# 48 more first-layer steps behind the last product, in eight groups that read their columns in different orders and from different begins

## The chip, the cores and the metric

The kernel runs on one core of a Trainium2 chip. Times are device microseconds of that core; lower is better. The engines are called as the profile calls them: PE (TensorE, with PEld for its weight loads), DVE (VectorE), ACT (ScalarE), POOL (GpSimd) and SP (SyncE, which issues DMAs here).

## The reference

A depthwise convolution over time is followed by a layer with a hard-swish gate:

```python
w = softmax(weight)                      # 8 heads x 7 taps
y[b, s, d] = sum_k w[head(d), k] * x_padded[b, s + k, d]   # 8 x 4096 x 192
h = y.reshape(32768, 192) @ w_in         # 192 x 2048
g = h * clip(h + 3, 0, 6) / 6
out = g @ w_out                          # 2048 x 192
```

All results are float32.

## The kernel before

The 32768 tokens are cut into 32 blocks of 1024, and a block into two halves of 512 columns. The 192 channels are laid on 96 partitions times two parts, so that with `y_own` and `y_other` two times 64 rows (`D2`) of TensorE's array are filled: rows 0 to 63 with one token half, rows 64 to 127 with the other.

**First layer** (`first_layer`, and `products` at L436 to L446). For each of 8 chunks of 128 hidden channels (twice, for the two groups) and each of three thirds (`s`) there are three passes, (high, high), (low, high) and (high, low). Weights and `y` are each kept as a high and a low part in the type fp32r, and `PASSES` names which parts meet. One **step** is one round of the inner loop over `k`: two matmuls that use 64 rows each, 128 weight columns and 512 moving columns, and write two neighbouring banks of PSUM. Each matmul comes with a weight load. `relu` on ACT (L315) and `gate` on DVE (L319) take the banks out.

**Second layer** (`second_layer`). It computes `g @ w_out` by sums and products of quarter matrices, in column tiles of 32 (`tile_position=(0, j * QS)`), so that four streams of f32 matmuls (L582, recorded by the helper `matmul`) run beside each other. Its order is written out by hand: `put` and `do` give each event a time on one of four streams, and the events are issued in order of that time. It takes three of the four PSUM slots (two banks each), `d, e, b, c, a, x_`, and the two banks `ends` of the fourth. In the last block (`last`) `end_lower` and `end_upper` turn the final rows and store them through the queues of SP, ACT and POOL.

**PSUM slots.** `free_slots` is the list of slots that are not taken. At the end of `second_layer` the three are given back behind the one that stayed, in this order:

```python
        free_slots.extend(ours[n] for n in (0, 2, 1))
```

so that behind the last block `free_slots[1]` is the slot of `d` and `e`.

**Weights of the first layer.** `w_in_parts` (L122) are two tiles, the high and the low part, with 8 x 3 x 128 = 3072 float32 columns per partition. They are written once in the first stage (L229 and L230) and then only read.

**The whole.** The first block is prepared in the first stage, with convolution taps on PE (`pe_tap`, L923: f32, 128 rows, 512 columns that begin at column k of `x0`), and its second layer is done plainly (L330). Blocks 1 to 31 follow in the loop over `i`, each a first layer and a second layer. TensorE's program is in the order in which the code issues it; all of this stands under `manual_schedule`. At the end of the program (L1162) all engines meet twice: each drains and counts up a semaphore, POOL waits for the count and lets the others go.

Of the kernel before, what the change touches and what calls it, by code (L numbers as in the profile page):

```python
# [1132 lines left out]
            left = second_layer(i, between)  # L1133


# [1 line left out]
_INS = ['x', 'weight', 'moe_w_in', 'moe_w_out']  # L1137
_OUTS = [((32768, 192), 'float32')]
# [28 lines left out]
```

## Time and profile before

| what | value |
|---|---|
| runs of the kernel | 2195.53, 2195.55, 2195.72 us; median 2195.55 |
| the profiled execution | 2195.85 us |
| its span, first to last instruction | 2194.1 us |
| granted TensorE clock | 1.000 |
| first-layer matmuls (L442) | 9216, in 4608 steps |
| second-layer matmuls (L582), largest group | 5720 |
| the last store's landing | about 2192.2 us |

The profile records each instruction's start and end. Matmuls overlap, and their ends are modelled; so the pace of TensorE is read from the distance between starts and not from the length of one. Groups of instructions have their line, engine, operation, output and inputs, shape and number. PEld are the weight loads, which run beside the matmuls of the step before. Entries whose engine ends in q (SPq, POOLq, PEldq) are records of an engine's sequencer: waits, drains and the issue of DMAs.

### The profile page before, as it was taken

To read this page: it belongs to the slowest core of one execution; us is meant where nothing else is said; L and a number is where in the kernel's file an instruction comes from. 1 tells how busy PE (TensorE), PEld (TensorE's weight loads), DVE (VectorE), ACT (ScalarE), POOL (GpSimd) and SP (SyncE) were. 2 spreads that over 40 slices of the span, in tenths; PEclk is the share of its full clock that TensorE was granted. 3 is DMA by queue.
4 is the path that set the end of the run, shared out by engine and by line. 5 is a ranking of instruction groups with operands and counts; after the bars stand their busy time and mean duration, and the time that the engine had idled before them with its cause. 6 is when DMAs were issued, how large, how long until landed. Compare 5 with 4: busy or idle time off the path is not lost.

```text
span 2194.1 us, 53702 instructions
## 1 busy us (share of the span) xinstructions
PE 2185.0 (100%) x23086; PEld 1565.5 (71%) x23086; DVE 1976.1 (90%) x1871; ACT 1270.9 (58%) x1761; POOL 1012.9 (46%) x859
## 2 busy tenths in 40 slices
PE   9999999999999999999999999999999999999998
PEld 5577777777777777777777777777777777777776
DVE  8889899889899898998989988999989999999987
ACT  7456565565655665555656556565566565565654
POOL 3445543355433555334554335553355543455433
PEclk9999999999999999999999999999999999999999
DMA  7366556756567665666655675656666566755564
GB/s 166 66 119 100 97 99 111 128 90 107 97 111 121 103 109 92 109 112 121 98 97 100 112 126 91 106 97 113 120 107 106 91 109 112 122 96 97 100 104 63
DMA packets 329821, 231.80 MB, mean 106 GB/s; under 512 B 208816, under 2 KB 293296, under 8 KB 329584
## 3 DMA queue, kind: packets, MB, share of 16 engines
q0 software_dynamic: 98752, 122.35, 36.6%
q1 hardware_dynamic: 229320, 105.73, 23.9%
q8 instruction: 181, 2.97, 0.6%
q10 hardware_dynamic: 1512, 0.30, 0.1%
q14 instruction: 56, 0.46, 0.1%
HBM read 31.72 MB, written 25.17 MB: 26 GB/s over the span
## 4 chain that ended last, share of the span: by engine, by line
PE 99%; ACT 0%; DVE 0%; POOL 0%; issue 0%; POOLq 0%; DVEq 0%
PE psum L582 49%; PE psum L442 47%; PE psum L330 2%; PE psum L923 0%; PE psum L931 0%; ACT g L315 0%; DVE results L409 0%; POOL w_in L230 0%; ACT scale L207 0%; ACT sig L204 0%; POOL out_dram L356 0%; ACT sig L210 0%; POOL sig L221 0%; DVE xt L832 0%; ACT w_in L229 0%
## 5 line engine op out<-in xcount | busy, mean ns | idle before, releaser
L582 PE MATMUL psum<-g,w_out 128*32 128x512 f32 (+1 forms) x5720 | 1023.7, 508 | 0.0
L315 ACT ACTIVATE g<-psum,half 128x1024 f32<-128x1024 f32 x512 | 571.3, 1116 | 313.5 <-PE psum L442 311.3
L582 PE MATMUL psum<-s,w_out 128*32 128x512 f32 (+1 forms) x3272 | 735.6, 570 | 0.9 <-DVE results L409 0.9
L319 DVE SCALAR_TENSOR_TENSOR g<-g,psum 128x1024 f32<-128x1024 f32 x512 | 609.1, 1211 | 134.3 <-ACT g L315 133.9
L540 POOL TENSOR_TENSOR s<-g 128x256 f32<-128x256 f32 x248 | 257.2, 1037 | 750.9 <-DMA out_dram<-results 639.6
L582 PEld LDWEIGHTS psum<-g,w_out 128*32 128x32 f32 x5720 | 421.0, 110 | 171.5 <-issue 61.6
L442 PE MATMUL psum<-y,w_in 64*128 64x512 f32 x4608 | 534.3, 388 | 0.4
L442 PE MATMUL psum<-y_other,w_in 64*128 64x512 f32 x4608 | 528.7, 386 | 0.0
L442 PEld LDWEIGHTS psum<-y,w_in 64*128 64x128 f32 x4608 | 428.6, 184 | 120.9 <-issue 26.0
L442 PEld LDWEIGHTS psum<-y_other,w_in 64*128 64x128 f32 x4608 | 431.6, 184 | 90.7
L1006 DVE SCALAR_TENSOR_TENSOR y<-x,c_sb,y 128x1536 f32<-128x1536 f32 x156 | 305.1, 1956 | 1.9 <-ACT y L1003 1.8
L582 PEld LDWEIGHTS psum<-s,w_out 128*32 128x32 f32 x3272 | 227.5, 110 | 106.3 <-issue 54.0
L582 PE MATMUL psum<-g,w_s 128*32 128x256 f32 x1488 | 289.3, 379 | 0.0
L389 POOL TENSOR_TENSOR s<-g 128x1024 f32<-128x1024 f32 x93 | 236.9, 2715 | 0.4 <-DVE g L319 0.4
L582 PE MATMUL psum<-z,w_s 128*32 128x256 f32 x992 | 235.1, 380 | 0.0
L389 DVE TENSOR_TENSOR s<-g 128x1024 f32<-128x1024 f32 x124 | 187.5, 1531 | 1.1
L582 PEld LDWEIGHTS psum<-g,w_s 128*32 128x32 f32 x1488 | 149.9, 110 | 31.9
L582 PE MATMUL psum<-s,w_s 128*32 128x256 f32 x744 | 170.7, 379 | 0.0
L482 ACT ACTIVATE z<-g 128x512 f32<-128x512 f32 x186 | 142.5, 766 | 18.4 <-DVE g L319 18.4
L409 DVE TENSOR_TENSOR g<-g 128x1024 f32<-128x1024 f32 x124 | 143.6, 1219 | 1.1
L409 DVE TENSOR_TENSOR results<-psum,results 32x256 f32<-32x256 f32 (+2 forms) x221 | 107.9, 488 | 39.6 <-PE psum L582 34.2
L389 DVE TENSOR_TENSOR g<-g 128x2048 f32<-128x2048 f32 x62 | 139.4, 2286 | 1.0
(114 smaller groups left out, 2335.2 us busy)
## 6 DMA issues: line engine op xcount, KB each, us to landing
y_other<-y SPq DMA_DIRECT2D x124, 384.0 KB, 5.1
z<-g POOLq DMA_DIRECT2D x93, 512.0 KB, 5.6
z<-z POOLq DMA_DIRECT2D x62, 512.0 KB, 5.4
out_dram<-results SPq DMA_DIRECT2D x375, 64.0 KB, 2.6
y<-x POOLq DMA_DIRECT2D x30, 768.0 KB, 9.0
x<-in_x_dram SPq DMA_DIRECT2D x53, 388.5 KB, 7.3
g<-g POOLq DMA_DIRECT2D x31, 512.0 KB, 6.3
g<-in_moe_w_in_dram SPq DMA_DIRECT2D x16, 192.0 KB, 5.8
```

The lines of the kernel that those rows point to most:

```text
L315: nc.scalar.activation(r6, h, ACT.Relu, bias=half[:], scale=1.0 / 6.0)
L319: nc.vector.scalar_tensor_tensor(out=g_, in0=g_, scalar=1.0, in1=h, op0=ALU.min, op1=ALU.mult)
L330: lambda p=p: nc.tensor.matmul(out=bank[j * QS : (j + 1) * QS, tokens], lhsT=w_out[:, p, w, cols], rhs=x[:, p, tokens], start=(first and p ...
L389: engine.tensor_tensor(out=o[:, r], in0=a[:, r], in1=b[:, r], op=op)
L409: nc.vector.tensor_tensor(out=out, in0=x, in1=y, op=op)
L442: nc.tensor.matmul(out=psum[:, 2 * slot + k], lhsT=r32(w_in_parts[wn][r, c, s]), rhs=r32(y_other[0][r, yn, s] if group else y_own[yn][r, s ...
L482: nc.scalar.mul(to, x, sign)
L540: engine.tensor_tensor(out=o, in0=p, in1=q, op=op)
L582: nc.tensor.matmul(out=out, lhsT=w, rhs=x, start=start, stop=True, tile_position=(0, j * QS), skip_group_check=True,)
L1006: nc.vector.scalar_tensor_tensor(out=y[:], in0=taps_of(k), scalar=c_sb[:, k : k + 1], in1=y[:], op0=ALU.mult, op1=ALU.add,)
```

## The change

Behind the loop over the blocks, 48 steps are added: eight groups of six, and in each step the two matmuls of 64 rows. The weights are always the same 128 columns of the high part, from column 24 on. The moving operand is 512 columns of the low part, which begin at column 24 plus `ahead`, in the order that `form` gives. Without a form the 512 columns are read one after the other. With `by_line` the columns are seen as runs of 16 (64 bytes), and the read goes over every b-th run, b times with another first run: with b of 4, 2 or 8 it steps over 256, 128 or 512 bytes from one run to the next. The last form reads every sixteenth column, 32 of them, sixteen times. The results are written into both banks of `free_slots[1]`, are sums of nothing else (`start` and `stop` are set in each), and are read by nobody. What is computed before stays as it is.

```diff
+        high, low = (w[:].rearrange("p c s f -> p (c s f)") for w in w_in_parts)
+        aligned = 24
+        spare = 2 * free_slots[1]
+
+        def columns(r, ahead, form):
+            c = low[r, aligned + ahead : aligned + ahead + N]
+            if form is None:
+                return c
+            pattern, sizes = form
+            return c.rearrange(pattern, **sizes)
+
+        by_line = "p (j b a) -> p b j a"
+        for ahead, form in (
+            (0, None),
+            (0, (by_line, dict(b=4, a=16))),
+            (0, (by_line, dict(b=2, a=16))),
+            (0, (by_line, dict(b=8, a=16))),
+            (32, None),
+            (48, None),
+            (16, (by_line, dict(b=4, a=16))),
+            (0, ("p (j a) -> p a j", dict(a=16))),
+        ):
+            for _ in range(6):
+                for k in range(2):
+                    r = slice(k * D2, (k + 1) * D2)
+                    nc.tensor.matmul(
+                        out=psum[:, spare + k], lhsT=r32(high[r, aligned : aligned + P]),
+                        rhs=r32(columns(r, ahead, form)),
+                        start=True, stop=True, skip_group_check=True,
+                    )
```

## Prediction

> **What bounds the kernel now.** I read the page first, its parts 1 and 4.
>
> ```profile
> span 2194.1 us, 53702 instructions
> PE 2185.0 (100%) x23086; PEld 1565.5 (71%) x23086; DVE 1976.1 (90%) x1871; ACT 1270.9 (58%) x1761; POOL 1012.9 (46%) x859
> PE 99%; ACT 0%; DVE 0%; POOL 0%; issue 0%; POOLq 0%; DVEq 0%
> ```
>
> TensorE is busy from end to end and makes up 99% of the chain that ended last. So what TensorE is given in the middle lengthens the span one for one. The change gives it work at the very end, though, where this share says nothing: there I need the last microseconds. The timeline of TensorE has its last products:
>
> ```profile
> 2187.12 0.39 PE L582 MATMUL psum<-s,w_out 128*32 128x256 f32 x3
> 2187.14 0.38 PE L582 MATMUL psum<-g,w_out 128*32 128x256 f32 x1
> 2187.34 0.39 PE L582 MATMUL psum<-s,w_out 128*32 128x256 f32 x3
> 2187.36 0.38 PE L582 MATMUL psum<-g,w_out 128*32 128x256 f32 x1
> ```
>
> Columns are start and length in us. The last product begins at 2187.36 and ends, as modelled, at 2187.73. The span ends at 2194.07, so 6.3 us follow in which TensorE has nothing to do. The chain, in order of time, and the records of the kernel's last line (L1162, where the engines meet) say what fills them:
>
> ```profile
> 2187.75 0.49 POOL out_dram L356
> 2188.24 0.09 issue
> 2188.33 0.58 POOL out_dram L356
> 2188.91 0.78 POOLq L1162
> 2189.69 0.53 POOL out_dram L356
> ```
>
> ```profile
> L1162 SPq EVENT_SEMAPHORE  x10: 17/28/1780, 2190.2 to 2194.0; - x10
> L1162 POOLq DRAIN  x3: 46/93/4281, 2188.8 to 2193.6; - x3
> L1162 SPq DRAIN  x3: 7/7/7, 2192.5 to 2193.3; - x3
> L1162 PEldq DRAIN  x2: 13/786/1560, 2186.3 to 2193.4; - x2
> ```
>
> (Shortest, median and longest in ns, then first and last start.) The last rows of the output are transposed and stored until 2190.2; SP then waits 1.78 us for stores to land, and its drain ends at 2192.54. GpSimd's first drain takes 4.281 us, from 2188.78 to 2193.06. TensorE's drain ends at 2187.84, 0.10 behind its last product. All engines are counted into one meeting that GpSimd closes: its wait begins at 2193.11, and 0.96 us later, with a second meeting in between, the span is over. So **TensorE arrives 5.2 us before the meeting**. That is the cover for whatever is put behind its last product.
>
> **The change, part by part.** It adds 48 steps. Each is two matmuls of 64 rows, 512 columns and 128 weight columns, with two weight loads: 96 matmuls and 96 loads, all on TensorE. It adds no DMA, no eviction and no store, and removes and moves nothing. All of it stands behind the last product in TensorE's program, so nothing is queued behind it but TensorE's drain.
>
> *Does the first one wait?* Its banks are those of the first of the three slots that the last block took, `d` and `e`. Their last readers are ACT's copies around L740 and L705 and DVE's at L409, from 2171.2 to 2173.1 in the timeline, 14 us before. `high` and `low` have been in place since the first 64 us. I cost the waits at nothing; without that cover the price would be what is left of such a copy, 0.4 us at most.
>
> *What is one step?* The first layer's steps have the same shape and number type. The timeline of TensorE inside and at the begin of a first layer:
>
> ```profile
> 2121.71 3.11 PE L442 MATMUL psum<-y,w_in 64*128 64x512 f32 x26
> ```
>
> ```profile
> 499.09 0.62 PE L582 MATMUL psum<-s,w_out 128*32 128x512 f32 x3
> 499.21 0.59 PE L582 MATMUL psum<-g,w_out 128*32 128x512 f32 x1
> 499.73 1.20 PE L442 MATMUL psum<-y,w_in 64*128 64x512 f32 x8
> ```
>
> 26 matmuls are 13 steps. Less the last one's own 0.386 and the 3 ns between the two of a step, 2.72 us hold 12 intervals: **226.5 ns a step**, and the starts in the trace say 226 or 227 in nearly all of 4608. At the begin it is slower: the last product of L582 started at 499.21 and takes 0.43 for its 512 columns, so the first step at 499.73 comes 0.09 later than the next product would have. The steps then start 337, 236, 228, 232 and 231 ns apart before the even pace holds; every later block shows the same five.
>
> *The sum with eight groups at this pace.* The last product has 256 columns and rounds of it start 0.215 apart, so the first new step starts at 2187.36 + 0.21 + 0.09 = 2187.66. Five slow intervals are 1.26 and 42 at 226.5 ns 9.51, so the last one starts at 2198.44 and ends 0.39 later, at 2198.83. The drain follows at +0.10, the meeting closes 0.04 behind it (as behind GpSimd's drain now), and 0.96 remain: 2199.93. Against 2194.07 that is **+5.9 us**: 11.1 us of TensorE's time, 5.2 of which lie beside the stores. SP may have to wait for the last added matmul before its drain, as nobody else reads its bank; from SP's last wait to the end of its drain it is 0.13 now, so at most 0.1 more. The stores themselves now have over 6 us to spare.
>
> A rule of the Trainium skill bears on the step (TensorE: Matmul & The Clock Gate, section "Wait — 56ns, not 53.3ns?"): once warm, matmuls start their columns divided by 2.4 GHz plus some 2.5 ns apart, 215.7 ns for 512. The row has 226.5, and the row decides; by the rule the sum would be 0.5 us less.
>
> *What do order and begin of the columns change?* No matmul in this trace reads its columns in another order, so I bound it. Groups 1, 5 and 6 read 512 neighbouring columns and differ in where they begin by 128 and 192 bytes. The nearest rows are the convolution taps on TensorE (L923), each one column further on than the one before: their matmuls start 428 to 433 ns apart with no more to it. Between nothing and 5 ns a step; I take nothing (12 steps would make 0.06 us). Groups 2, 3, 4 and 7 (the last begins 64 bytes further on) read runs of 16 columns (64 bytes) with 64 to 448 bytes skipped between them. Lower bound: the f32 products pass 512 columns in 429 ns; were a step twice as fast it would take 214.5, 12 less than it does, and an order that loses those 12 would give back 0.3 us over 24 steps. Upper bound: such a read goes at the pace of the f32 products, 429, which is 4.9 us over 24 steps. I take 226.5: if the 12 ns are lost at 32 changes from one 64-byte run to the next, 0.375 ns each (an estimate from these two rows), these groups change just as often. Group 8 takes every sixteenth column, so each column lies in another run than the one before. By that estimate 512 changes cost 192 ns, giving 406; the nearest row is the f32 pace, 429. Bounds: 226.5 below, and above it the 857 that a whole tap takes on L923 (two matmuls of 428). I take 429, **6 steps × 202 ns = +1.2 us**.
>
> The skill has a rule on this read, too (SBUF — State Buffer, in the box on cachelines; Advanced Engine Details and Errata, "SBUF Cachelines"): SBUF gives full bandwidth only where at least two accesses in a row fall into one 16-byte line. It speaks against group 8 alone, since runs of 64 bytes meet it, and states no price; no run here shows it yet.
>
> **Sum:** 5.9 + 1.2 = 7.1 us. The profiled execution took 2195.85, 1.75 beyond its span, and the median of the runs shown is 2195.55, 0.30 less; what lies around the span doesn't change. 2195.55 + 7.1 = **2202.6 us**, 0.32% more. About 0.2% (4.4 us) is what a measurement can tell from no change here, so slower by more than that begins at 2199.9.
>
> **Rivals.**
>
> 1. *The order isn't felt:* all 48 steps take 226.5 or, without the surplus, 214.5. For it: the taps' begin hardly shows, and the step's time has been the same to a nanosecond whatever tile was read. Against it: something costs 12 ns a step. 2195.55 + 5.9 = 2201.4, or with 48 × 12 ns off 2200.8. Chance 0.2.
> 2. *Group 8 costs much more than half pace*, at 857 a step: 6 × 630 = 3.8 in place of 1.2, so 2205.2. For it: 64 bytes of stride, twice as many runs to touch as any row shows per column. Against it: no row at full clock goes that slowly in a single matmul. Chance 0.17.
> 3. *Skipping runs costs too:* groups 2, 3, 4 and 7 at 429, so 4.9 on top of 7.1: 2207.5. For it: the reads jump. Against it: as many runs are opened as in a plain read. Chance 0.08.
> 4. *The end doesn't wait for the added steps,* and the time stays 2195.55: nobody evicts their banks, and if only the stores' landings and the engines that make them hold the end, 11 us of TensorE lie outside the span. What decides is whether TensorE's drain stands behind its matmuls in the meeting. Against it: that drain ends 0.10 behind the last product now, with its count going to the semaphore on which GpSimd waits. Chance 0.04, the only case that isn't slower.
>
> The forecast, even pace for seven groups and about half pace for the eighth, keeps 0.51. For the range, 2200.7 is the low end of rival 1 and 2205.5 that of rival 2 with SP's 0.1 and the 5 ns of begin; 0.12 lie outside by rivals 3 and 4. Slower by over 0.2% in all cases but the fourth: 0.95 with a little off for a cover that is longer than I see; within 0.2% 0.04, faster 0.01.
>
> **What the changed profile would show.** L442's lines stay as they are; the diff's line has 96 matmuls and 96 loads. First start at 2187.66; starts 226 to 227 ns apart in groups 1 to 7 behind five slower ones, 406 to 429 in group 8; the last product's end, 2187.73, and the stores as now; TensorE's drain at 2200.1 and the last to arrive; 0.96 us behind it to a span of 2201.2. I would be wrong by a first step that waits beyond 2187.7, by runs that cost something when skipped, by a group 8 outside 400 to 450, or by an end that comes before TensorE's drain.

## The result, and the profile after

The changed kernel takes **2203.18 us** (median of 6 runs, 2203.03 to 2203.28), against 2195.54 before (6 runs): 7.64 us more, a ratio of 1.0035 with a 95% interval of 1.0022 to 1.0048. The forecast was 2202.6, in a range of 2200.7 to 2205.5. The profiled execution took 2203.09 us with a span of 2201.3, 7.25 us more than the span before.

The page of the changed kernel, its span, its busy line and the head of its chain:

```profile
span 2201.3 us, 53895 instructions
PE 2197.6 (100%) x23182; PEld 1575.1 (72%) x23182; DVE 1975.1 (90%) x1871; ACT 1271.8 (58%) x1761; POOL 1014.2 (46%) x859
PE 99%; ACT 1%; DVE 0%; POOL 0%; DMA 0%; issue 0%; DVEq 0%
```

TensorE has the 96 matmuls more and is busy for 12.6 us more; the span has grown by 7.25. The difference, 5.3 us, is taken to be the cover at the end; the experiments below test that. The chain in its last microseconds consists of nothing but TensorE now:

```profile
2185.87 1.73 PE psum L582 x32
2187.60 12.64 PE psum L1163 x96
```

Before, the stores through GpSimd were the last links. The timeline of TensorE at the seam, then inside groups 2, 3, 5, 6 and 8 (each line is one answer for a stretch within one group):

```profile
2187.20 0.39 PE L582 MATMUL psum<-s,w_out 128*32 128x256 f32 x3
2187.22 0.38 PE L582 MATMUL psum<-g,w_out 128*32 128x256 f32 x1
2187.53 1.65 PE L1163 MATMUL psum<-w_in,w_in 64*128 64x512 f32 x12
...
2189.25 1.36 PE L1163 MATMUL psum<-w_in,w_in 64*128 64x512 f32 x10
2190.69 1.36 PE L1163 MATMUL psum<-w_in,w_in 64*128 64x512 f32 x10
...
2193.50 1.32 PE L1163 MATMUL psum<-w_in,w_in 64*128 64x512 f32 x10
2194.90 1.33 PE L1163 MATMUL psum<-w_in,w_in 64*128 64x512 f32 x10
...
2197.48 2.76 PE L1163 MATMUL psum<-w_in,w_in 64*128 64x512 f32 x12
```

The first added step starts 0.31 behind the last product; 0.30 had been reckoned. Twelve matmuls of group 8 are six steps: less the 0.60 of the last one, 2.16 us hold five intervals, **431 ns each**. Ten matmuls of group 2 are five steps: less 0.40, 0.96 hold four, 240 each, and so on. From the starts in the trace, per group: the first six intervals of group 1 are 337, 236, 228, 232, 231 and 227 ns, as at the begin of the first layers to within 2 ns; groups 2 and 3 have 239 on average, 4 and 5 231, 6 and 7 235, and 8 has 431.

The records of the last line show who closes the meeting:

```profile
L1196 POOLq DRAIN  x3: 46/102/5965, 2188.6 to 2200.8; - x3
L1196 SPq DRAIN  x3: 7/7/7, 2200.3 to 2200.6; - x3
L1196 PEldq DRAIN  x2: 13/1989/3965, 2196.3 to 2200.7; - x2
```

GpSimd's first drain ends at 2194.61 (2188.65 and 5.965), those of VectorE and ScalarE by 2190.6. TensorE's begins at 2196.33 and ends at 2200.29 (3.965). SP has one wait more than before (11 records for 10) and its drains end at 2200.28 and 2200.34, with TensorE's. GpSimd's wait begins at 2200.37 and the span is over 0.95 later.

### The profile page after: what moved, and what is told of

Read it like the earlier page. It is cut to its first block, busy times and chain, and to the rows that moved or that the text cites. A ratio compares the mean times of both kernels' runs of the same rounds, so it can differ in the third digit from the quotient of the medians.

```text
span 2201.3 us, 53895 instructions
## 1 busy us (share of the span) xinstructions
PE 2197.6 (100%) x23182; PEld 1575.1 (72%) x23182; DVE 1975.1 (90%) x1871; ACT 1271.8 (58%) x1761; POOL 1014.2 (46%) x859
## 4 chain that ended last, share of the span: by engine, by line
PE 99%; ACT 1%; DVE 0%; POOL 0%; DMA 0%; issue 0%; DVEq 0%
PE psum L582 49%; PE psum L442 47%; PE psum L330 2%; PE psum L1163 1%; PE psum L923 0%; PE psum L931 0%; ACT g L315 0%; DVE results L409 0%; DMA y_other<-y 0%; POOL w_in L230 0%; ACT scale L207 0%; ACT sig L204 0%; ACT sig L210 0%; POOL sig L221 0%; ACT w_in L229 0%; DVE s L389 0%
## 5 line engine op out<-in xcount | busy, mean ns | idle before, releaser
L582 PE MATMUL psum<-g,w_out 128*32 128x512 f32 (+1 forms) x5720 | 1023.8, 508 | 0.0
L582 PE MATMUL psum<-s,w_out 128*32 128x512 f32 (+1 forms) x3272 | 735.4, 570 | 0.9 <-DVE results L409 0.9
L582 PEld LDWEIGHTS psum<-g,w_out 128*32 128x32 f32 x5720 | 421.2, 110 | 171.9 <-issue 61.7
L582 PEld LDWEIGHTS psum<-s,w_out 128*32 128x32 f32 x3272 | 227.9, 110 | 106.8 <-issue 54.3
L582 PE MATMUL psum<-g,w_s 128*32 128x256 f32 x1488 | 289.3, 379 | 0.0
L582 PE MATMUL psum<-z,w_s 128*32 128x256 f32 x992 | 235.1, 380 | 0.0
L582 PEld LDWEIGHTS psum<-g,w_s 128*32 128x32 f32 x1488 | 149.8, 110 | 31.9
L582 PE MATMUL psum<-s,w_s 128*32 128x256 f32 x744 | 170.7, 379 | 0.0
L540 POOL TENSOR_TENSOR s<-s,g 128x256 f32<-128x256 f32 x124 | 136.3, 1100 | 9.7
```

The source lines that it names most:

```text
L540: engine.tensor_tensor(out=o, in0=p, in1=q, op=op)
L582: nc.tensor.matmul(out=out, lhsT=w, rhs=x, start=start, stop=True, tile_position=(0, j * QS), skip_group_check=True,)
```

## The experiments

Three of the kernels below (`seven`, `twenty`, `middle`) and the two with pads were run several times. Each kernel with a table of steps was run once, and its figures come from that one trace, at a granted clock of 1.000.

The theory at this point: TensorE gets 12.6 us more, 5.2 us of which lie beside the stores, and the step's price is set by how its columns are read. Its rivals: that the cover is none (the stores give way, or the end doesn't wait for TensorE); and, for the price of a read, other rules than the prediction's.

**Without the eighth group** (`seven`).

```diff
-            (0, ("p (j a) -> p a j", dict(a=16))),
```

> The change without its eighth group: 42 steps, groups 1 to 7 as they are. By the prediction's sum with the 431 ns that the profile of the changed kernel shows for a step of group 8, the time falls by 6 x 0.431 = 2.6 us to about 2200.6. If part of what group 8 costs were hidden, or the end did not wait for TensorE, it falls by less, or not at all.

Measured: 2200.56 us (10 runs; before beside it 2195.62), a ratio of 1.0023 (1.0013 to 1.0032). That is 2.62 less than the changed kernel, or 2.70 if each is taken against the kernel before beside it; six steps of 431 are 2.59. The intervals reach 2 to 3 us to each side, so the agreement to 0.1 us rests on the medians. Once the cover is used up, what is put at the end counts in full, and group 8 costs what its starts say.

**Twenty steps in place of 48** (`twenty`).

```diff
-        for ahead, form in (
...
-            for _ in range(6):
+        for _ in range(20):
...
+                    rhs=r32(low[r, aligned : aligned + N]),
```

> 20 plain steps behind the last product and nothing else. They take 0.31 to begin, 1.26 for five slow intervals, 14 x 0.2265 = 3.17 and 0.39 to end, so TensorE's drain comes some 4.9 us behind its present place, at 2192.7 to 2192.8, before GpSimd's drain (2193.06 in the kernel before). If those 5.2 us are cover, the time is that of the kernel before, 2195.5, within 0.2 us. Rival, the added steps lengthen the end by disturbing the stores or by one more wait of SP: 2196 or more. Rival, there is no cover: 2195.5 + 4.8 = 2200.3.

Measured: 2195.54 us (10 runs) against 2195.62, a ratio of 0.9999 (0.9990 to 1.0009): no change, although TensorE works 4.8 us longer. The records of that kernel's last line:

```profile
L1175 POOLq DRAIN  x3: 46/102/4111, 2188.7 to 2193.3; - x3
L1175 SPq DRAIN  x3: 7/7/7, 2192.4 to 2193.1; - x3
L1175 PEldq DRAIN  x2: 13/1348/2682, 2189.8 to 2193.1; - x2
```

TensorE's drain ends at 2192.44 (2189.75 + 2.68), and GpSimd's 4.111 us from 2188.68 end at 2192.79, still last. So TensorE lengthens the end only where it comes last; the kernel with 48 steps shows that it is awaited then.

**The same 48 steps in the middle** (`middle`).

```diff
             left = second_layer(i, between)
+            if i == 16:
...
```

> The same 48 steps, but behind the second layer of block 16 in place of the last one, where the first layer of block 17 follows and no store is waited for. If the 5.2 us of cover belong to the kernel's end alone, the whole length of the steps counts: 13.0 us from the first added start to the end of the last by the changed kernel's profile, less what the following first layer would have paid itself for its slow begin, so +12.4 to +12.9 and 2208 to 2208.5. Rival, other engines use the pause to catch up and TensorE waits less later: TensorE waits for others only 1.3 us in all its second layers, so at most that much comes back, 2207. Rival, a pause of TensorE in front of ACT and DVE costs more than its own length, because their work comes later in a bunch: over 2209.

Measured: 2208.44 us (4 runs) against 2195.62, a ratio of 1.0058 (1.0043 to 1.0073): +12.8 against +7.6 at the end. The timeline of TensorE at both seams:

```profile
1174.01 0.59 PE L582 MATMUL psum<-g,w_out 128*32 128x512 f32 x1
1174.53 0.50 PE L1161 MATMUL psum<-w_in,w_in 64*128 64x512 f32 x2
...
1186.64 0.61 PE L1161 MATMUL psum<-w_in,w_in 64*128 64x512 f32 x2
1187.07 1.33 PE L442 MATMUL psum<-y,w_in 64*128 64x512 f32 x10
```

The 13.0 us of the expectation run from the start of the last product in the changed kernel; from the first added start to the last end it is 12.7 there and here. From 1174.53 to 1187.07 the following first layer waits 12.54 us, and every later block starts 12.5 to 12.6 later than in the kernel before. Neither rival shows: nothing is caught up, nothing is bunched. The difference between the medians, 12.8 and 7.6, is 5.2, the cover; the single runs of `middle` spread by 0.6 us, so it is not known to the tenth.

**What a read that jumps costs** (`strides`): eight groups of 24 steps.

```diff
+        for a in (1, 2, 4, 8, 16, 32, 64, 1):
+            for _ in range(24):
...
+                    c = low[r, aligned : aligned + N]
...
+                        rhs=r32(c if a == 1 else c.rearrange("p (j a) -> p a j", a=a)),
```

> Eight groups of 24 steps behind the last product, in place of eight groups of 6. Each reads the same 512 columns, every a-th of them, with a = 1, 2, 4, 8, 16, 32, 64 and again 1. Read is the distance between starts in the later half of each group. Theory of the prediction (a surplus of 0.375 ns for each change of 64-byte run, on a floor of 214.5 ns): 226.5 at a = 1, 238 at 2 (64 changes), 262 at 4, 310 at 8, 406 or a little more at 16, 32 and 64, so a slope. Rival, two accesses in a row must fall into one 16-byte line (the Trainium skill, SBUF - State Buffer, box on cachelines): 226 at 1 and 2, and one step up to the 431 measured for group 8 already at 4, the same for 8, 16, 32 and 64. Second rival, the price depends on how far the read jumps: 431 at 16 and more than that at 32 and 64. The last group shows whether the pace of a plain read drifts with its place: 226.5 again if it doesn't.

Measured, ns a step (mean of the later half of each group, from the starts in the trace): 

| every a-th column | 1 | 2 | 4 | 8 | 16 | 32 | 64 | 1 |
|---|---|---|---|---|---|---|---|---|
| ns | 226.6 | 453.6 | 461.3 | 431.2 | 433.5 | 434.8 | 486.7 | 226.7 |

The timeline in the groups with a of 2, 4, 8 and 16:

```profile
2194.92 3.35 PE L1144 MATMUL psum<-w_in,w_in 64*128 64x512 f32 x14
2205.82 3.41 PE L1144 MATMUL psum<-w_in,w_in 64*128 64x512 f32 x14
2216.78 3.63 PE L1144 MATMUL psum<-w_in,w_in 64*128 64x512 f32 x16
2227.13 3.65 PE L1144 MATMUL psum<-w_in,w_in 64*128 64x512 f32 x16
```

(Seven steps in the first two, eight in the others; the last one's own length is 0.63, 0.64, 0.61 and 0.61.) The slope of the prediction's theory, 238 at 2 and 262 at 4, isn't there, and the rule of the Trainium skill (SBUF — State Buffer, in the box on cachelines) that two accesses in a row to a 16-byte line suffice fails for these fp32r steps: with a = 2 each line is met twice in a row and the step takes double. It is one step up, at the first jump. A price for each line opened isn't it either: at a = 2 half as many lines are opened as at a = 4, and the step takes as long. The last group, 226.7, excludes a drift with the place. Theory of the prediction and rival both fall here; of the second rival, the distance, the 486.7 at 64 alone could be left, since 2 and 4 cost more than 8 to 32. What makes these differences stays open.

**How long a run must be** (`runs_of`): every fourth run of a columns, with different begins.

```diff
+        for ahead, a in ((0, 16), (0, 2), (1, 2), (2, 2), (3, 2), (0, 4), (2, 4), (0, 8), (0, 32), (0, 64)):
...
+                        rhs=r32(c.rearrange("p (j b a) -> p b j a", b=4, a=a)),
```

> Ten groups of 24 steps behind the last product. Every fourth run of a neighbouring columns is read, four times with another first run, so the read jumps after each run; (begin, a) = (0,16) (0,2) (1,2) (2,2) (3,2) (0,4) (2,4) (0,8) (0,32) (0,64). Reads in which no two neighbours follow each other took 431 to 487 ns, at every second column as at every sixteenth. Theory pair, one access every two cycles brings two neighbours that lie in the same 8 bytes: 226 to 245 with a = 2 at begin 0 and 2, and about 431 or more at begin 1 and 3; all longer runs 226 to 245. Theory line, an access brings what lies in the same 16 bytes if it is asked for in a row: 226 to 245 with a = 2 at begin 0, 1 and 2, and 431 at begin 3; (2,4) in between. Theory form, what counts is that the innermost step is one column, whatever its length: all between 226 and 245. Theory length, short runs cost per run (64-byte runs cost 4 to 13 ns for 32 runs, so 0.1 to 0.4 ns each): a = 8 about 235 to 252, a = 4 about 240 to 278, a = 2 about 252 to 330.

| begin, run | 0, 16 | 0, 2 | 1, 2 | 2, 2 | 3, 2 | 0, 4 | 2, 4 | 0, 8 | 0, 32 | 0, 64 |
|---|---|---|---|---|---|---|---|---|---|---|
| ns | 238.5 | 461.3 | 461.4 | 460.0 | 460.0 | 225.7 | 455.7 | 229.9 | 233.3 | 226.6 |

The timeline in the groups (0, 2), (0, 4) and (2, 4):

```profile
2195.53 2.95 PE L1144 MATMUL psum<-w_in,w_in 64*128 64x512 f32 x12
2239.73 2.86 PE L1144 MATMUL psum<-w_in,w_in 64*128 64x512 f32 x24
2245.17 2.92 PE L1144 MATMUL psum<-w_in,w_in 64*128 64x512 f32 x12
```

(Six, twelve and six steps in nearly the same time.) All four theories miss something. Runs of two cost double wherever they begin (against "pair" and "line"), runs of four are free if they begin at a multiple of 16 bytes and cost double if they lie across two such lines (against "form" and "length"). What fits all eighteen groups of the two kernels: **the full pace of these fp32r reads needs all four columns of a 16-byte line in a row**; where fewer are taken at once, the step takes about twice as long (431 to 487).

**The same with f32** (`f32_strides`), in the second layer's form: four matmuls beside each other in column tiles of 32.

```diff
+        for ahead, a in ((0, 1), (0, 2), (0, 4), (0, 16), (0, 64), (1, 1), (8, 1), (48, 1)):
+            for _ in range(12):
+                for j in range(4):
+                    c = low[:, aligned + ahead : aligned + ahead + N]
+                    nc.tensor.matmul(
+                        out=psum[rows(j), spare], lhsT=w_out[:, 0, B11, 0:QS],
+                        rhs=c if a == 1 else c.rearrange("p (j a) -> p a j", a=a),
+                        start=True, stop=True, tile_position=(0, j * QS), skip_group_check=True,
+                    )
```

> Eight groups of 12 rounds behind the last product, in the form of the second layer's products: four f32 matmuls beside each other in column tiles of 32, 128 rows, 512 columns, all reading the same tile. Every a-th column or another begin: (begin, a) = (0,1) (0,2) (0,4) (0,16) (0,64) (1,1) (8,1) (48,1). Theory, f32 takes a column every two cycles anyway and four streams share what a read delivers: if a read that jumps costs two cycles per column as in the fp32r steps, it is hidden, and all groups take 429 to 435 ns a round. Rival, the price is on the read and comes on top or four streams add up: 640 to 860 at a = 2, 4 and 16, and more where fp32r was slower too (a = 64). Begin: nothing, at most 5 ns, as with the taps of the convolution.

Each f32 matmul is two instructions, so a round has two sets of four; the expectation spoke of a round where it meant a set. Measured, ns a set (mean of the later half of each group):

| begin, a | 0, 1 | 0, 2 | 0, 4 | 0, 16 | 0, 64 | 1, 1 | 8, 1 | 48, 1 |
|---|---|---|---|---|---|---|---|---|
| ns | 429 | 455 | 900 | 891 | 868 | 429 | 429 | 429 |

The timeline in the groups with a of 2 and 4, four sets each:

```profile
2199.36 2.02 PE L1143 MATMUL psum<-w_in,w_out 128*32 128x512 f32 x16
2211.14 3.81 PE L1143 MATMUL psum<-w_in,w_out 128*32 128x512 f32 x16
```

Here every second column is nearly free (6%), and from every fourth on, one column per line, the time doubles. The theory "hidden" nearly holds at a = 2 alone. From 4 on there is a price on top, as the rival says, but a little above its 640 to 860, and a = 64 is not the slowest. So for f32 the trace agrees with the rule of the Trainium skill (Advanced Engine Details and Errata, "SBUF Cachelines"): at least two hits on a 16-byte line are needed. For fp32r, whose columns pass twice as fast, it takes four. The two tests differ in more than the type, though: the f32 matmuls have 128 rows and run four beside each other, the fp32r ones have 64 rows and run two. Which of these sets the number was not tried.

**Whether the begin is felt** (`begins`): nine groups of neighbouring columns.

```diff
+        for ahead in (0, 1, 4, 8, 16, 32, 48, 64, 0):
+            for _ in range(24):
...
+                        rhs=r32(low[r, aligned + ahead : aligned + ahead + N]),
```

> Nine groups of 24 steps behind the last product, all of 512 neighbouring columns, which begin 0, 1, 4, 8, 16, 32, 48, 64 and again 0 columns behind column 24 of the low part. In the changed kernel groups 5 and 6 (32 and 48 columns further on) ran at 231 and 235 ns a step and not at 226.5. Theory A, the begin is felt: 226.5 at 0, about 231 at 32, about 235 at 48, and 226.5 again in the last group. Theory B, the begin is not felt (the prediction's price of nothing), and what made those groups slower is the stretch behind another group or where they stand: all nine at one value, or slower the later they stand, the last like its neighbours. Theory C, it is something of the added steps that the first layer's lack (weights and columns from neighbouring tiles, the same weights each time): all nine near 231 to 235 once the slow first steps are over, the first and the last as well.

| begin | 0 | 1 | 4 | 8 | 16 | 32 | 48 | 64 | 0 |
|---|---|---|---|---|---|---|---|---|---|
| ns | 226.6 | 236.5 | 232.0 | 233.2 | 228.6 | 232.9 | 233.3 | 226.6 | 226.6 |

Theory A: the begin counts, and 64 columns, 256 bytes, are as good as none. B and C fall with the last group. But the first layer runs at 226.5 with columns that begin 160 bytes behind a multiple of 256 (by the layout of the tiles; the traces have no addresses), which isn't explained yet.

**Begin of columns against begin of weights** (`pairs_of_begins`).

```diff
+        for ahead, w_ahead in ((0, 0), (40, 0), (40, 40), (0, 40), (8, 8), (0, 8), (24, 0), (24, 24), (48, 48), (1, 1), (12, 0), (56, 0)):
...
+                    w_at = aligned + w_ahead
...
+                        out=psum[:, spare + k], lhsT=r32(high[r, w_at : w_at + P]),
+                        rhs=r32(low[r, aligned + ahead : aligned + ahead + N]),
```

> Twelve groups of 24 steps behind the last product, 512 neighbouring columns each. Columns begin c and weights w columns behind column 24 of their tiles (which lies at a multiple of 256 bytes); (c, w) = (0,0) (40,0) (40,40) (0,40) (8,8) (0,8) (24,0) (24,24) (48,48) (1,1) (12,0) (56,0). Before, with w = 0: 226.6 ns a step at c = 0 and 64, 228.6 to 236.5 at 1, 4, 8, 16, 32 and 48. In the first layer weights and columns both begin 160 bytes behind a multiple of 256, which is 40 columns, at 226.5. Theory D, it is the distance between the two begins, modulo 256 bytes: 226.6 wherever c = w, (40,40), (8,8), (24,24), (48,48) and (1,1) too; slower by 2 to 10 in (40,0), (0,40), (0,8), (24,0), (12,0), (56,0). Theory M, the begin of the columns alone: (40,0) and (40,40) both at 226.6 as in the first layer, (0,40) and (0,8) at 226.6, (8,8) at 233 and (48,48) at 233 as with w = 0, (1,1) at 236.5.

| columns, weights | 0,0 | 40,0 | 40,40 | 0,40 | 8,8 | 0,8 | 24,0 | 24,24 | 48,48 | 1,1 | 12,0 | 56,0 |
|---|---|---|---|---|---|---|---|---|---|---|---|---|
| ns | 226.7 | 234.4 | 226.6 | 232.9 | 226.6 | 233.2 | 233.0 | 226.6 | 226.6 | 237.6 | 233.5 | 233.2 |

The timeline in the groups (40,0), (40,40) and (0,40), ten steps each:

```profile
2195.26 2.51 PE L1144 MATMUL psum<-w_in,w_in 64*128 64x512 f32 x20
2200.83 2.43 PE L1144 MATMUL psum<-w_in,w_in 64*128 64x512 f32 x20
2206.35 2.49 PE L1144 MATMUL psum<-w_in,w_in 64*128 64x512 f32 x20
```

The same columns take 9 intervals in 2.12 us or in 2.04 as the weights begin elsewhere or with them. Theory D holds for eleven of the twelve pairs: it is the distance between the two begins modulo 256 bytes. M falls with (40,0), (0,40), (8,8) and (48,48). One pair misses: (1,1), which begins 4 bytes behind a 16-byte line, takes 237.6 though the distance is nought.

**The distance in the kernel itself**, without any added step: a pad in front of y (`pad_y`), then a pad in front of all tiles (`pad_all`).

```diff
+    yo.tile([P, 8], F32, name="pad")
     y_own, z_early = own_tiles("y"), []
```

```diff
+    cst.tile([P, 8], F32, name="pad")
     w_sb = cst.tile([P, KC], F32, name="w_sb")
```

> The kernel before, without added steps, with 32 unused bytes in front of the tiles of y in SBUF: the columns of the first layer begin 192 in place of 160 bytes behind a multiple of 256, the weights stay at 160. If the begin (or its distance from the weights' begin) costs a real step what it cost an added one, 233.2 in place of 226.6 ns, 4608 steps take 30 us more and the time is about 2226. If the effect belongs to the added steps alone: 2195.5.

> The kernel before, without added steps, with 32 unused bytes in front of the first tile, so that weights and y both move to 192 bytes behind a multiple of 256, and all other tiles with them. Theory D (the distance between the begins of weights and columns counts): 2195.5, no change. Theory M (the columns' own begin counts): about 2226, as with the pad in front of y alone. If the products of the second layer feel a begin too, its 13456 matmuls show it, more than either.

Measured: 2224.43 us with the pad in front of y (4 runs; 2195.53 before), a ratio of 1.0131 (1.0114 to 1.0148), and 2195.51 (10 runs) with the pad in front of everything, 1.0001 (0.9992 to 1.0010). Groups of the first layer before, and in `pad_y`, whose lines are one further on:

```profile
L442 PE MATMUL psum<-y,w_in 64*128 64x512 f32 x4608 | 534.3, 388 | 0.4
L442 PE MATMUL psum<-y_other,w_in 64*128 64x512 f32 x4608 | 528.7, 386 | 0.0
...
L443 PE MATMUL psum<-y,w_in 64*128 64x512 f32 x4608 | 548.6, 394 | 0.1
L443 PE MATMUL psum<-y_other,w_in 64*128 64x512 f32 x4608 | 544.1, 392 | 0.0
```

Together they take 29.7 us more; the steps are 233.3 ns apart on average, against 226.9 (all distances under 300 ns counted). 32 bytes cost 29 us of 2195, and 32 bytes in front of both change nothing that can be told. The second layer's f32 products, L582 before and L583 here, feel neither: their largest group is busy for 1023.7 us before, 1023.6 and 1023.9.

**What the 12 ns of a step belong to** (`shapes`).

```diff
+        for m, n, rows_, w_at, ws, xs_ in (
+            (P, N, 64, aligned, high, low),
+            (P // 2, N, 64, aligned, high, low),
+            (QS, N, 64, aligned, high, low),
+            (P, N, 64, other, high, low),
+            (P, N, 64, aligned, low, high),
+            (P, N // 2, 64, aligned, high, low),
+            (P, 384, 64, aligned, high, low),
+            (P, N, 128, aligned, high, low),
+            (P, N, 64, aligned, high, low),
+        ):
```

> Nine groups of 24 steps behind the last product, with plain columns from column 24, to see what the 12 ns of a step belong to beyond the 214.5 that half an f32 product takes: (1) the added step as it is; (2) 64 weight columns; (3) 32 weight columns; (4) the 128 weight columns from 384 columns further on; (5) weights from the low and columns from the high part; (6) 256 columns; (7) 384 columns; (8) one matmul of 128 rows in place of two of 64; (9) as (1) again. Theory A, the surplus belongs to the columns read (32 runs of 64 bytes): 226.5 in 1 to 5 and 9, 113 in 6 and 170 in 7, 226.5 in 8. Theory B, it belongs to the weight load: 2 and 3 fall towards 214.5, 8 as well since it has half as many loads, and 6 and 7 keep the 12 ns (119 and 173). Theory C, it belongs to two row halves running beside each other: only 8 falls to about 214.5. In 6 the two weight loads of a step (184 ns each as the profile shows them, one behind the other or not) may set the pace in place of the columns: then it is well over 119.

| group | 1 | 2 | 3 | 4 | 5 | 6 | 7 | 8 | 9 |
|---|---|---|---|---|---|---|---|---|---|
| ns | 226.6 | 230.0 | 231.7 | 226.6 | 226.6 | 120.0 | 173.3 | 226.6 | 226.6 |

From 256 to 384 and from 384 to 512 columns it is 53.3 ns each, 0.417 a column; so 512 columns are 213.3 and a step has **13.3 ns that go with the step and not with its columns** (120.0 less 106.7, as many). That is theory B in groups 6 and 7. But a price that goes with the size or the number of the weight loads it isn't: fewer weight columns make a step slower, not faster, and one matmul of 128 rows, with one load, takes as long as two of 64 beside each other. A step without any load was not run. A, which the prediction used, falls, C as well. What the 13.3 ns are stays open.

## Why the prediction was right, and where a step of it failed

**The cover of 5.2 us** held. With 20 steps nothing is added, at the end 48 steps cost 7.6 and in the middle 12.8. Rival 4, an end that doesn't wait for TensorE, falls with the changed kernel's last records.

**The seam, the slow first steps and the even pace** held: 0.31 to begin, then 337, 236, 228, 232, 231 and 227, and 226.6 once it is even (the first group of `strides`). The waits that were costed at nothing weren't there.

**Begin of the columns: the step failed.** I took nothing, with at most 5 ns a step. Groups 5 and 6 took 231 and 235, 4 to 9 ns more, since their columns lie 128 and 192 bytes from the weights modulo 256. The row that I took for the nearest, the taps of the convolution, is f32, and the f32 products run here don't feel a begin (429 at 0, 1, 8 and 48).

**Skipped runs: the step was too low,** inside its bounds. 226.5 was taken and 231 to 239 measured, which the prediction had named as a sign of being wrong. Groups 2 to 7 cost together 0.3 us beyond the even pace. The span shows half of that (7.25 measured, 7.1 forecast), because the last product itself starts 0.14 earlier in this profiled execution than in the one of before, 2187.22 against 2187.36; all first layers of this execution begin 0.14 to 0.36 earlier too, so that has nothing to do with the steps. Runs of 64 columns go at 226.6 and those of 4 to 32, begun on a 16-byte line, between 226 and 239; why that is so for each length stays open.

**Group 8: the size was right, its working wrong.** 429 was taken and 431 measured. But the estimate behind it, 0.375 ns for each change of a 64-byte run, asked for 238 ns at every second column, where it is 454; and the 12 ns that it shared out over the runs belong to the step. The f32 row, at half the pace, was the better guide, but the prediction had no reason why a read that jumps should go at just that pace: other strides took 454, 461 and 487, so the fit to 2 ns is luck. Rival 1 (the order isn't felt) and rival 2 (857) fall with group 8's starts, rival 3 (429 for skipped runs) with groups 2 to 4 and 7.

**The median's remainder.** 7.64 between the medians against 7.24 between the two profiled executions is run-to-run spread: the profiled one of before was 0.31 above its median, that of the changed kernel 0.09 below.

## What to carry to other kernels

Work behind an engine's last instruction was free here as far as the other engines' way to the end reached, 5.2 us; read that from the drains of the last line, not from the busy share. The fp32r steps kept their pace where their moving operand took all four columns of a 16-byte line in a row (226 to 239 ns), and took about double from the first jump on where it didn't (431 to 487). Where fp32r weights and moving columns both began at the same place modulo 256 bytes, and on a 16-byte line, a step took 226.6 ns and elsewhere mostly 233, 3% more. So one small tile in front of `y` cost 1.3% of this kernel: look at the addresses before the schedule.

## What the runs showed that I had not expected

The last three stores land later behind a longer program: the last of them at 2193.70 in the changed kernel against 2192.16 before, although they are issued as before. In that stretch a block of instructions is fetched. The DMA views between 2189 and 2195, first of the kernel before, then of the changed one, which alone has the line of q8:

```profile
out_dram<-results ACTq DMA_DIRECT2D x2, 32.0 KB, 1.8
out_dram<-results SPq DMA_DIRECT2D x2, 32.0 KB, 1.9
...
q8 instruction: 1, 0.02, 1.7%
...
out_dram<-results ACTq DMA_DIRECT2D x2, 32.0 KB, 2.7
out_dram<-results SPq DMA_DIRECT2D x2, 32.0 KB, 2.8
```

The last figure is the median time in us from issue to landing. The block, 16384 bytes from 2190.74 on, occupies its DMA engine for 1.59 us. With 42 steps such a block is fetched too, in 1.02 us; with 20 steps there is none beside the stores. (A smaller one, of 8192 bytes, is fetched behind the last landing in all these kernels.) From the end of the last store's issue to its landing it takes 1.65 us before, 1.55 with 20 steps, 2.77 with 42 and 3.30 with 48. The cover hid it; that the block is the cause was not tried by itself.

Fewer weight columns make an fp32r step slower: 230.0 ns with 64 and 231.7 with 32, against 226.6 with 128.
